# Two leading token blocks of 256, opening loads in order of need, and a copy of W_in within SBUF

## The chip, the cores and the metric

The kernel runs on one core of a Trainium2 chip. The metric is the device time in microseconds. The span of a profile (first to last instruction) is about 1.8 us shorter than the time that is reported for the same run. A ratio is the mean time of one kernel's fast runs over the mean of the other kernel's fast runs of the same rounds, so it is not quite the ratio of the medians that are quoted.

## The reference

The reference is a causal convolution of 7 taps per token and head, then a two-layer network with exact GELU, on 32,768 tokens of 192 channels.

```python
w = softmax(weight)                         # 8 heads x 7 taps
out[b, s] = sum_k w[head, k] * x_pad[b, s + k]   # zeros before the start of each sequence
h = out.reshape(32768, 192) @ w_in          # 192 x 2048
g = 0.5 * h * (1 + erf(h / sqrt(2)))
return g @ w_out                            # 2048 x 192
```

## The kernel before

The 32,768 tokens are two halves of 16,384. A block takes 512 tokens of each half; the two halves lie in partitions 0-63 and 64-127, and so every TensorE instruction comes in pairs that run side by side (in the trace of this kernel the two of a pair start 3 to 4 ns apart; the 512-column ones take 376 ns each). There are 32 blocks. For each block the sync engine loads `x`; VectorE transposes it (3 steps), convolves it (21 steps: 7 taps times 3 groups of 64 channels) and writes `xc` as bf16; TensorE multiplies with W_in, 128 columns at a time ("first matmuls"); ScalarE applies GELU; TensorE multiplies with W_out ("second matmuls"); VectorE evicts the result; the sync engine stores it.

Stage n, in this document, is TensorE's pass that has the first matmuls of block n and, between them, the second matmuls of block n - 1. A slice is the part of a stage that belongs to one ScalarE call of 1,024 elements.

```python
# GpSimd: W_in (cast to bf16) after three instructions that build `sel`; then W_out
for c0, c1, s in ((0, FC, S_WIN[0]), (FC, F, S_WIN[1])):      # FC = 512 of F = 2048 columns
    for hf in range(2):                                        # lower and upper 64 partitions
        g.dma_start(win[64*hf.., c0:c1], w_in[..]).then_inc(s, 16)
g.dma_start(wout, w_out).then_inc(S_WOUT, 16)
# ...
# VectorE: block 0 alone, then block n + 1 with the evictions of block n - 1 between its steps
for op in ops0: run(0, op)
for n in range(NSB + 1):
    if n >= 2: evac(n - 2, 3)
    # ... 24 steps of block n + 1 in three parts, evac(n - 1, 0..2) after each
# ScalarE: one call per slice
a.wait_ge(S_MM1, u + 1)
a.activation(out=gT[n % 2][:, i*2*TB:(i+1)*2*TB], in_=hp[u % 2][:, :], func=AF.Gelu)
# TensorE
for n in range(NSB):
    for i in range(NF):                       # 16 slices
        mm1(n, i)                             # 6 matmuls, 512 columns
        if n >= 1: mm2_run(n - 1, ...)        # 16 matmuls
t.wait_ge(S_GELU, NF * NSB)                   # all of the last block, then its second matmuls
# ...
# Sync: the taps' weights, then x of blocks 0, 1, 2 ... without waiting
sp.dma_start(wsb, weight)
load(0); load(1)
# ... load(n + 2) and the stores
```

(Cuts are marked with `# ...`; access patterns are shortened.)

Of the kernel before, what the change touches and what calls it, by code (L numbers as in the profile page):

```python
# [11 lines left out]
def bass_lightweight_conv__then__act_gelu_exact_kernel(  # L12
# [16 lines left out]
    TB = 512  # L29
    assert B % 2 == 0 and SEQ % TB == 0  # L30
    NSB = HALF // TB
    SPB = SEQ // TB
# [3 lines left out]
    MB = TB // 32  # L36
# [4 lines left out]

# [6 lines left out]
    outt = out.tensor  # L48

# [14 lines left out]
    with es:  # L64
# [10 lines left out]
        xin = [sbt("xin%d" % i, [128, MB * XC], F32) for i in range(NX)]  # L75
# [9 lines left out]
        S_WIN = [sem("S_WIN%d" % i) for i in range(2)]  # L85
        S_WOUT = sem("S_WOUT")
        S_XIN = [sem("S_XIN%d" % i) for i in range(NX)]
        S_OUT = [[sem("S_OUT%d_%d" % (i, j)) for j in range(2)] for i in range(2)]
# [19 lines left out]
        def _(g):  # L108
            g.memset(sel[:, :], 1.0).then_inc(S_SEL)
# [21 lines left out]
            for c0, c1, s in ((0, FC, S_WIN[0]), (FC, F, S_WIN[1])):  # L131
                for hf in range(2):
                    g.dma_start(  # L133
                        ap(win, 64 * hf * NP * F + c0, [[NP * F, 64], [F, NP], [1, c1 - c0]]),
                        ap(wint, c0, [[F, 64], [64 * F, NP], [1, c1 - c0]]),
                    ).then_inc(s, 16)
# [4 lines left out]
            for n in range(NSB):  # L141
                dst = ap(xT[n % 2], 0, [[NP * XW, 128], [XW, NP], [1, HL]])
                if n >= 2:
                    g.wait_ge(S_CV, NCV * (n - 1))
                if n % SPB == 0:
                    g.memset(dst, 0.0).then_inc(S_HALO)  # L146
                else:
                    g.wait_ge(S_TR, NP * n)
                    g.tensor_copy(  # L149
                        dst,  # L150
                        ap(xT[(n - 1) % 2], TB, [[NP * XW, 128], [XW, NP], [1, HL]]),
                    ).then_inc(S_HALO)

        @block.vector
        def _(v):
# [16 lines left out]
            def trans(n, p):  # L172
                if p == 0:
                    v.wait_ge(S_XIN[n % NX], 64 * (n // NX + 1))  # L174
                    if n >= 2:
                        v.wait_ge(S_CV, NCV * (n - 1))
                    if n >= 1:
                        v.wait_ge(S_HALO, n)
                v.transpose(  # L179
                    ap(xT[n % 2], p * XW + HL, [[NP * XW, 128], [1, TB]]),  # L180
                    ap(xin[n % NX], 64 * p, [[MB * XC, 128], [XC, MB], [1, 32]]),
                ).then_inc(S_TR)

            def conv(n, k, p):
                if k == 0 and p == 0:
                    v.wait_ge(S_TR, NP * (n + 1))
                    v.wait_ge(S_HALO, n + 1)
                idx = NCV * n + NP * k + p
                if idx >= NP:
                    v.wait_ge(S_CV, idx - NP + 1)  # L190
                src = ap(xT[n % 2], p * XW + k, [[NP * XW, 128], [1, TB]])
                w = wcol[:, p * KS + k : p * KS + k + 1]
                a = acc[:, p * TB : (p + 1) * TB]
                if k == 0:
                    ins = v.tensor_scalar(a, src, w, None, ALU.mult)  # L195
                else:
                    dst = a
                    if k == KS - 1:
                        dst = xc[n % 2][:, p * TB : (p + 1) * TB]
                        if n >= 2 and p == 0:  # L200
                            v.wait_ge(S_MM1, NF * (n - 1))
                    ins = v.scalar_tensor_tensor(  # L202
                        dst, src, w, a, op0=ALU.mult, op1=ALU.add
                    )
                ins.then_inc(S_CV)

            def evac(m, g):
                v.wait_ge(S_MM2, 4 * m + g + 1)
                if m >= 2 and g % 2 == 0:
                    v.wait_ge(S_OUT[m % 2][g // 2], 16 * (m // 2))  # L210
                v.tensor_copy(  # L211
                    ap(osb[m % 2], 2 * g * C, [[8 * C, 128], [C, 2], [1, C]]),
                    ap(ob[g % 2], 0, [[1024, 128], [512, 2], [1, C]]),
# [14 lines left out]
            for n in range(NSB + 1):  # L228
                ops = list(ops0) if n + 1 < NSB else []
                cut = [0, 9, 17, 24, 24]  # L230
                if n >= 2:
                    evac(n - 2, 3)
                for q in range(4):
                    for op in ops[cut[q] : cut[q + 1]]:
                        run(n + 1, op)
                    if n >= 1 and q < 3:
                        evac(n - 1, q)
            evac(NSB - 1, 3)

        @block.scalar  # L240
        def _(a):
            a.wait_ge(S_PRO, 1)
# [7 lines left out]
            for n in range(NSB):  # L250
                for i in range(NF):
                    u = n * NF + i
                    a.wait_ge(S_MM1, u + 1)
                    if i == 0 and n >= 2:
                        a.wait_ge(S_MM2, 4 * (n - 1))
                    a.activation(  # L256
                        out=gT[n % 2][:, i * 2 * TB : (i + 1) * 2 * TB],
# [5 lines left out]
        def _(t):  # L263
# [8 lines left out]
            ins.then_inc(S_PEP)  # L272

            def mm1(n, i):
                u = n * NF + i
# [4 lines left out]
                if n == 0 and i == 0:  # L280
                    t.wait_ge(S_WIN[0], 32)
                if n == 0 and 128 * i == FC:
                    t.wait_ge(S_WIN[1], 32)
                for p in range(NP):
                    for hf in range(2):
                        r = slice(64 * hf, 64 * hf + 64)
                        ins = t.matmul(  # L287
                            hp[u % 2][:, hf * TB : (hf + 1) * TB],
                            win[r, p * F + 128 * i : p * F + 128 * i + 128],
                            xc[n % 2][r, p * TB : (p + 1) * TB],  # L290
                            start=(p == 0),
                            stop=(p == NP - 1),
                            tile_position=(64 * hf, 0),
                        )
                ins.then_inc(S_MM1)

            def mm2_run(m, g, ph, i0, i1):


                if g >= 2 or m >= 1:  # L300
                    if ph == 0 and i0 == 0:
                        t.wait_ge(S_EV, 4 * m + g - 1)
                if ph == 1 and i0 == 0:
                    t.wait_ge(S_PH, 4 * m + g + 1)
                for i in range(i0, i1):
                    for hf in range(2):
                        sub = ph ^ hf
                        s = 2 * g + sub
                        r = slice(64 * hf, 64 * hf + 64)
                        c0 = i * 2 * TB + s * 128  # L310
                        ins = t.matmul(  # L311
                            ob[g % 2][:, 512 * sub : 512 * sub + C],
                            gT[m % 2][r, c0 : c0 + 128],
                            wout[r, i * C : (i + 1) * C],
                            start=(ph == 0 and i == 0),
                            stop=(ph == 1 and i == NF - 1),
                            tile_position=(64 * hf, 0),
                        )
                if i1 == NF:
                    ins.then_inc(S_MM2 if ph == 1 else S_PH)  # L320

            for n in range(NSB):
                for i in range(NF):
                    mm1(n, i)
                    if n >= 1:
                        if n == 1 and i == 0:
                            t.wait_ge(S_WOUT, 16)
                        if i < 2:
                            t.wait_ge(S_GELU, NF * (n - 1) + 8 * (i + 1))
                        g, r = divmod(i, 4)  # L330
                        mm2_run(n - 1, g, r // 2, 8 * (r % 2), 8 * (r % 2) + 8)
            m = NSB - 1
            t.wait_ge(S_GELU, NF * NSB)
            for g2 in range(2):
                for ph in range(2):
                    for g in range(2):
                        mm2_run(m, 2 * g2 + g, ph, 0, NF)

        @block.sync
        def _(sp):  # L340
            sp.dma_start(wsb[:, :], ap(wt, 0, [[KS, H], [1, KS]])).then_inc(S_WSB, 16)  # L341

            def load(n):
                if n >= NX:
                    sp.wait_ge(S_TR, NP * (n - NX + 1))
                for q in range(4):
                    off = ((q // 2) * HALF + n * TB) * D + 32 * (q % 2)
                    sp.dma_start(  # L348
                        ap(xin[n % NX], 32 * q * MB * XC, [[MB * XC, 32], [XC, MB], [1, XC]]),
                        ap(xt, off, [[D, 32], [32 * D, MB], [1, XC]]),  # L350
                    ).then_inc(S_XIN[n % NX], 16)

            def store(m, hf):
                sp.wait_ge(S_EV, 4 * m + 2 * hf + 2)
                sp.dma_start(
                    ap(outt, (hf * HALF + m * TB) * C, [[C, 128], [128 * C, 4], [1, C]]),
                    ap(osb[m % 2], hf * 4 * C, [[8 * C, 128], [C, 4], [1, C]]),
                ).then_inc(S_OUT[m % 2][hf], 16)

            load(0)  # L360
            load(1)
            for n in range(NSB + 2):
                if n + 2 < NSB:
# [3 lines left out]
                if 1 <= n <= NSB:  # L367
                    store(n - 1, 0)
            for s in range(2):
                for hf in range(2):  # L370
                    sp.wait_ge(S_OUT[s][hf], 16 * ((NSB + 1 - s) // 2))

# [27 lines left out]
```

## Time and profile before

| | before |
|---|---|
| time, median of the 4 runs taken beside the changed kernel | 712.8 us (712.34 to 714.07) |
| span of the profiled run | 710.9 us |
| first transpose of block 0 | 14.84 us |
| first W_in matmul | 30.06 us |
| stage 1 starts (steady state) | 47.27 us |
| stage 2 starts | 68.20 us |

Two lines of the page: busy time of each engine with its share of the span, and the shares of the chain of work that ended last.

```profile
PE 676.3 (95%) x11270; PEld 487.9 (69%) x11270; DVE 544.5 (77%) x901; ACT 526.2 (74%) x516; POOL 18.2 (3%) x44
PE 94%; DVE 2%; DMA 2%; ACT 2%; issue 0%; SPq 0%; DVEq 0%
```

PE is TensorE, DVE is VectorE, ACT is ScalarE, POOL is GpSimd. TensorE sets the time, and only the rest, about 35 us (710.9 - 676.3), can be won without changing its work. The timeline shows where that rest lies. Its columns are the start (us), the length (us), engine, line, operation, output and inputs with their shapes, the number of instructions merged, and in brackets the idle time before them and what ended it.

```profile
14.84 1.90 DVE L179 STREAM_TRANSPOSE xT<-xin 128x512 f32<-128x512 f32 x3 [9.67 <-DMA xin<-in_x_dram]
16.78 1.30 DVE L195 TENSOR_SCALAR acc<-xT,wcol 128x512 f32<-128x512 f32 x3
18.00 10.02 DVE L202 SCALAR_TENSOR_TENSOR acc<-xT,wcol,acc 128x512 f32<-128x512 f32 x15
27.93 2.07 DVE L202 SCALAR_TENSOR_TENSOR xc<-xT,wcol,acc 128x512 bf16<-128x512 f32 x3
30.06 7.26 PE L287 MATMUL hp<-xc,win 64*128 64x512 bf16 x36 [25.10 <-DVE xc L202]
...
68.20 0.81 PE L287 MATMUL hp<-xc,win 64*128 64x512 bf16 x6
...
694.50 0.81 PE L287 MATMUL hp<-xc,win 64*128 64x512 bf16 x6
695.14 0.82 PE L311 MATMUL ob<-wout,gT 64*128 64x192 bf16 x16
696.43 10.73 PE L311 MATMUL ob<-wout,gT 64*128 64x192 bf16 x256 [0.46 <-ACT gT L256]
```

VectorE waits 9.67 us for block 0's `x`, works 15.2 us on it, and only then has TensorE something to do. From 68.20 us a slice follows a slice every 1.3075 us, (694.50 - 68.20) / 479, to the end. The windows view gives busy time by stretch; the columns after the length are busy us and instruction count of PE, PEld (weight loads), DVE, ACT and POOL, then the granted clock, the DMA share and GB/s.

```profile
15.00:30.06 15.06, 0.00 (x1) 0.01 (x2) 15.02 (x25) 0.00 (x0) 0.20 (x1) 1.00 1.26 224
30.06:36.50 6.44, 6.38 (x30) 1.58 (x31) 6.41 (x12) 4.11 (x5) 0.45 (x1) 1.00 1.22 195
36.50:47.30 10.80, 9.06 (x68) 2.35 (x70) 10.77 (x18) 10.78 (x12) 0.31 (x1) 1.00 0.14 24
47.30:68.20 20.90, 20.90 (x352) 15.21 (x354) 14.29 (x24) 16.63 (x17) 0.14 (x1) 1.00 0.43 82
```

In the second row TensorE is busy all the time with only 30 matmuls, 5 slices of 1.29 us; a slice of first matmuls alone takes 0.65 us later. I read this as half clock: the slices take twice as long, as does one of 1.28 us in the changed kernel's trace (46.26 to 47.54 us), where the clock record reads 0.50. The column of the granted clock still reads 1.00 there, because the trace's first clock record of this run is at 36.07 us. In the third row ScalarE is busy throughout and sets the pace, and in the fourth TensorE is.

### The profile page before, as it was taken

To read this page: it belongs to the slowest core of one execution; us is meant where nothing else is said; L and a number is where in the kernel's file an instruction comes from. 1 tells how busy PE (TensorE), PEld (TensorE's weight loads), DVE (VectorE), ACT (ScalarE), POOL (GpSimd) and SP (SyncE) were. 2 spreads that over 40 slices of the span, in tenths; PEclk is the share of its full clock that TensorE was granted. 3 is DMA by queue.
4 is the path that set the end of the run, shared out by engine and by line. 5 is a ranking of instruction groups with operands and counts; after the bars stand their busy time and mean duration, and the time that the engine had idled before them with its cause. 6 is when DMAs were issued, how large, how long until landed. Compare 5 with 4: busy or idle time off the path is not lost.

```text
span 710.9 us, 24500 instructions
## 1 busy us (share of the span) xinstructions
PE 676.3 (95%) x11270; PEld 487.9 (69%) x11270; DVE 544.5 (77%) x901; ACT 526.2 (74%) x516; POOL 18.2 (3%) x44
## 2 busy tenths in 40 slices
PE   0389999999999999999999999999999999999997
PEld 0037777777777777777777777777777777777776
DVE  2987897777789777779877778977777887777711
ACT  1197777777777777777777777777777777777771
POOL 3000000000000000000000000000000000000000
PEclk9999999999999999999999999999999999999999
DMA  9915533555543455554345555335555433551012
GB/s 188 216 25 119 98 85 83 99 120 121 98 106 86 76 118 121 120 98 94 86 86 120 120 114 98 88 82 102 120 121 98 104 87 75 120 121 46 24 47 68
DMA packets 104390, 71.04 MB, mean 100 GB/s; under 512 B 5216, under 2 KB 103904, under 8 KB 104288
## 3 DMA queue, kind: packets, MB, share of 16 engines
q1 hardware_dynamic: 101392, 67.12, 45.5%
q0 software_dynamic: 2896, 2.36, 2.1%
q8 instruction: 88, 1.44, 0.9%
q14 instruction: 14, 0.11, 0.1%
HBM read 46.66 MB, written 25.17 MB: 101 GB/s over the span
## 4 chain that ended last, share of the span: by engine, by line
PE 94%; DVE 2%; DMA 2%; ACT 2%; issue 0%; SPq 0%; DVEq 0%
PE ob L311 47%; PE hp L287 46%; DMA xin<-in_x_dram 2%; ACT gT L256 2%; DVE acc L202 1%; DVE xT L179 0%; SPq L348 0%; DVE acc L195 0%; DVE xc L202 0%; DVE osb L211 0%; SPq L341 0%; DVEq L174 0%
## 5 line engine op out<-in xcount | busy, mean ns | idle before, releaser
L256 ACT ACTIVATE gT<-hp 128x1024 bf16<-128x1024 f32 x512 | 523.2, 1023 | 169.1 <-PE hp L287 169.1
L287 PE MATMUL hp<-xc,win 64*128 64x512 bf16 x3072 | 417.7, 378 | 26.9 <-DVE xc L202 25.1
L311 PEld LDWEIGHTS ob<-wout,gT 64*128 64x128 bf16 x8192 | 352.6, 94 | 118.2 <-ACT gT L256 0.7
L311 PE MATMUL ob<-wout,gT 64*128 64x192 bf16 x8192 | 419.2, 243 | 0.5 <-ACT gT L256 0.5
L202 DVE SCALAR_TENSOR_TENSOR acc<-xT,wcol,acc 128x512 f32<-128x512 f32 x480 | 325.6, 747 | 0.0
L287 PEld LDWEIGHTS hp<-xc,win 64*128 64x128 bf16 x3072 | 141.3, 94 | 97.3 <-DVE xc L202 25.2
L211 DVE COPY osb<-ob 128x384 f32<-128x384 f32 x128 | 71.0, 555 | 148.2 <-PE ob L311 148.2
L179 DVE STREAM_TRANSPOSE xT<-xin 128x512 f32<-128x512 f32 x96 | 60.4, 681 | 9.7 <-DMA xin<-in_x_dram 9.7
L202 DVE SCALAR_TENSOR_TENSOR xc<-xT,wcol,acc 128x512 bf16<-128x512 f32 x96 | 66.4, 749 | 0.0
L195 DVE TENSOR_SCALAR acc<-xT,wcol 128x512 f32<-128x512 f32 x96 | 40.9, 483 | 1.1
L149 POOL COPY xT<-xT 128x18 f32<-128x18 f32 x28 | 12.3, 438 | 576.3 <-DVE xT L179 576.3
L267 PE MATMUL ob<-wnm,sel 8*128 8x7 f32 x6 | 1.4, 354 | 3.5 <-DVE wnm L165 3.5
L267 PEld LDWEIGHTS ob<-wnm,sel 8*128 8x128 f32 x6 | 1.4, 321 | 3.5 <-issue 3.5
L133 POOL DMA_DIRECT2D win<-in_moe_w_in_dram x4 | 2.6, 657 | 0.0
L243 ACT ACT_TABLE_LOAD x1 | 1.3, 1283 | 0.8 <-PEq L385 0.8
L157 DVE TENSOR_REDUCE wmx<-wsb 8x1 f32<-8x7 f32 x1 | 0.1, 148 | 2.2 <-DMA wsb<-in_weight_dram 2.2
L146 POOL MEMSET xT<- 128x18 f32 x4 | 0.5, 121 | 41.0 <-DVE xc L202 41.0
L169 DVE COPY wcol<-ob 128x21 f32<-128x21 f32 x1 | 0.2, 181 | 1.6 <-PE ob L267 1.6
L256 ACT ACT_TABLE_LOAD x1 | 1.3, 1283 | 0.0
L137 POOL DMA_DIRECT2D wout<-in_moe_w_out_dram x1 | 1.2, 1192 | 0.0
L112 POOL TENSOR_SCALAR_AFFINE_SELECT sel<-sel 8x384 f32<-8x384 f32 x1 | 0.5, 537 | 0.1
L122 POOL TENSOR_SCALAR_AFFINE_SELECT sel<-sel 8x384 f32<-8x384 f32 x1 | 0.5, 532 | 0.1
(10 smaller groups left out, 1.8 us busy)
## 6 DMA issues: line engine op xcount, KB each, us to landing
xin<-in_x_dram SPq DMA_DIRECT2D x128, 320.0 KB, 6.7
out_dram<-osb SPq DMA_DIRECT2D x64, 384.0 KB, 3.0
win<-in_moe_w_in_dram POOLq DMA_DIRECT2D x2, 576.0 KB, 12.7
wout<-in_moe_w_out_dram POOLq DMA_DIRECT2D x1, 768.0 KB, 22.7
win<-in_moe_w_in_dram POOLq DMA_DIRECT2D x2, 192.0 KB, 8.4
wsb<-in_weight_dram SPq DMA_DIRECT2D x1, 0.2 KB
```

The source lines that it names most:

```text
L133: g.dma_start(ap(win, 64 * hf * NP * F + c0, [[NP * F, 64], [F, NP], [1, c1 - c0]]), ap(wint, c0, [[F, 64], [64 * F, NP], [1, c1 - c0]]),) ...
L137: g.dma_start(ap(wout, 0, [[NF * C, 128], [C, NF], [1, C]]), ap(woutt, 0, [[C, 128], [128 * C, NF], [1, C]]),).then_inc(S_WOUT, 16)
L149: g.tensor_copy(dst, ap(xT[(n - 1) % 2], TB, [[NP * XW, 128], [XW, NP], [1, HL]]),).then_inc(S_HALO)
L179: v.transpose(ap(xT[n % 2], p * XW + HL, [[NP * XW, 128], [1, TB]]), ap(xin[n % NX], 64 * p, [[MB * XC, 128], [XC, MB], [1, 32]]),).then_i ...
L195: ins = v.tensor_scalar(a, src, w, None, ALU.mult)
L202: ins = v.scalar_tensor_tensor(dst, src, w, a, op0=ALU.mult, op1=ALU.add)
L211: v.tensor_copy(ap(osb[m % 2], 2 * g * C, [[8 * C, 128], [C, 2], [1, C]]), ap(ob[g % 2], 0, [[1024, 128], [512, 2], [1, C]]),).then_inc(S_EV)
L243: a.activation(out=wex[:, :], in_=wsb[:, :], func=AF.Exp, bias=wmx[:, 0:1], accum_out=wsm[:, 0:1],).then_inc(S_ACTP)
L256: a.activation(out=gT[n % 2][:, i * 2 * TB : (i + 1) * 2 * TB], in_=hp[u % 2][:, :], func=AF.Gelu,).then_inc(S_GELU)
L267: ins = t.matmul(ob[0][:, p * KS : (p + 1) * KS], sel[:, p * 128 : (p + 1) * 128], wnm[:, :],)
L287: ins = t.matmul(hp[u % 2][:, hf * TB : (hf + 1) * TB], win[r, p * F + 128 * i : p * F + 128 * i + 128], xc[n % 2][r, p * TB : (p + 1) * T ...
L311: ins = t.matmul(ob[g % 2][:, 512 * sub : 512 * sub + C], gT[m % 2][r, c0 : c0 + 128], wout[r, i * C : (i + 1) * C], start=(ph == 0 and i ...
```

## The change

The intent is to give TensorE its first work earlier. The first two blocks take 256 tokens per half; to keep ScalarE's calls at 1,024 elements, two 128-column chunks of W_in share one call. The loads are ordered by need: block 0's `x` alone on the sync queue, the taps' weights on ScalarE's, the first quarter of W_in first on GpSimd's; block 1's `x` waits for block 0's; the upper half of the rest of W_in is copied from the lower half within SBUF, ahead of block 2's `x`. Two further differences come with the rewriting: the evictions are placed differently between VectorE's steps, and TensorE's wait for the last block's activations is split into two halves.

```diff
+    WS = [256, 256] + [512] * ((HALF - 512) // 512)      # OFF, NCH, NSL, SL0, NG, G0 follow from it
 # GpSimd
+            for hf in range(2):                           # now ahead of the memset and the two selects
+                g.dma_start(win[64*hf.., 0:FC], w_in[..]).then_inc(S_WIN[0], 16)
             g.memset(sel[:, :], 1.0).then_inc(S_SEL)
 ...
-            for c0, c1, s in ((0, FC, S_WIN[0]), (FC, F, S_WIN[1])):
-                for hf in range(2): g.dma_start(...).then_inc(s, 16)
+            g.dma_start(win[lower 64.., FC:F], w_in[..]).then_inc(S_WIN[1], 16)
 # VectorE
-                cut = [0, 9, 17, 24, 24]
+                for g in range(ng):
+                    to = min(len(ops), (len(ops) * (g + 1) + ng - 2) // max(ng - 1, 1))
+                    ... steps of block n + 1 up to `to`, then evac(n - 1, g); the last one in the next stage
 # ScalarE
+            a.dma_start(wsb[:, :], ap(wt, 0, [[KS, H], [1, KS]])).then_inc(S_WSB, 16)
-                        out=gT[n % 2][:, i * 2 * TB : (i + 1) * 2 * TB],
+                        out=ap(gT[n % 2], i * c * 2 * w, [[NF * 2 * TB, 128], [w, 2], [2 * w, c], [1, w]]),
 # TensorE
+                for cc in range(c):                       # c = 2 chunks of W_in per slice in a small block
-            t.wait_ge(S_GELU, NF * NSB)                   # before the last second matmuls
+                    if i % max(c, 8) == 0: t.wait_ge(S_GELU, ...)   # for each half of the chunks
 # Sync
             load(0)
+            sp.wait_ge(S_XIN[0], 64)
             load(1)
+            sp.wait_ge(S_WIN[1], 16)
+            sp.dma_start(win[upper 64.., FC:F], win[lower 64.., FC:F]).then_inc(S_WIN[2], 16)
+            load(2)
```

## The prediction

> **What bounds the kernel now.** TensorE: the page gives PE 95% busy, the chain of waits puts 94% on it. In the timeline the steady stage (one block's first matmuls beside the previous block's second) takes 20.9 us, (694.7 - 47.3) / 31, PE without a gap, ScalarE about 16.4, VectorE 17.0. The change leaves that work as it is; what it can win lies before. VectorE waits until 14.84 us for block 0's x; transposes and convolution take 15.2 us; PE's first W_in matmul starts at 30.06; stage 0 starts with slices of 1.29 us, then runs at ScalarE's pace (a call per 0.97 us) to 47.3. The second steady stage starts at 68.2.
>
> **What the change does.**
> 1. Block 0's x is half as large and goes first. Before, its first 1,024 x packets, as many as the new block has, had landed at 7.1 us. Now its queue starts 0.5 us earlier, though W_in's packets begin near 4.4 us (3.6 after issue, as before). VectorE starts at about 6.8 instead of 14.8: -8 us.
> 2. Block 0 has 256 columns. VectorE steps at 512 are 0.631 (transpose), 0.433 (first tap), 0.668 us (later taps). [...] First matmul at about 16 us: -14.
> 3. Two small blocks cost 18.5 us of VectorE where one cost 15.2: +3.3 us. Block 2 (512) follows at 15.2. Until the steady state VectorE sets the pace. ScalarE's calls stay 1,024 wide.
> 4. Block 2's x queues behind block 1's and the SBUF copy of W_in. From the packet rates (300 per us alone, 220 beside W_out) I estimate landing near 27 us, when VectorE is free at 25.3-26: +1 to 1.5 us.
> 5. PE's small stages end near 37 us, but block 2 is convolved only at 42. [...] This trace shows 1.29 us slices for 6.4 us after the opening idle; I count 1.2 us for a partial repeat.
>
> **On the critical path.** Block 3's stage, the first steady one, starts at 6.8 + 18.5 + 1.5 + 15.2 = 42, plus stage 2 (block 3's convolution and two evictions, 16.4; ScalarE 15.5), plus 1.2 = about 59.8 us. From there 30 full stages and the tail remain, as after 68.2 before. Gain 8.4 us, not 14, because VectorE gives much back. The late copy of W_in (near 18.5 us) should hit the third slice of stage 0 and cost nothing: PE has slack there.
>
> **Predicted time:** 704.3 us, range 700.5 to 708.0. Faster by over 2%: 3%; within 2%: 96%; slower by over 2%: 1%. For 2% the steady state would have to start before 54 us; after a start at 6.8, two small and two large blocks (48.9 us of VectorE) do not allow it.
>
> **What would show it.** In the timeline: first transpose at 6-7.5 us; 256-wide taps spaced near 0.40 us; first W_in matmul at 15.5-17; PE waiting several us for VectorE before block 2, with slices of over 1 us after it; block 3's first matmul at 58-62; stages of 20.9 us after it; PE busy time nearly unchanged.
>
> **What would make it wrong.** x of block 1 or 2 landing much later; the copy or W_out landing after 25 us; [...] eviction order stalling the first second matmuls; 256-wide weight loads not hidden.

The sum came to 6.8 + 18.5 + 1.5 + 15.2 = 42.0 us, plus 16.4 for stage 2, plus 1.2 for its slow slices: 59.6, put as "about 59.8". The gain is 68.2 - 59.8 = 8.4 us, and 704.3 is 712.7 (the kernel before, median of the three runs then made) less 8.4. The 18.5 (two small blocks; with half of it the first matmul at about 16 us) and the spacing of 0.40 us were estimates; the changed kernel measured 18.6 us and 0.40 us. The 1.2 was from the 1.29 us slices; that the clock would fall after the gap was not shown by the trace at hand. Stage 2 then lost 1.2 to 1.3 us. The third cut is a case of what would make the forecast wrong.

## The result, and the profile after

| | before | after |
|---|---|---|
| time, median of 4 runs each | 712.8 us | 705.1 us (704.3 to 705.92) |
| ratio of the fast runs | | 0.9889, 95% interval 0.9871 to 0.9907 |
| span of the profiled run | 710.9 us | 702.9 us |
| first transpose | 14.84 us | 9.35 us |
| first W_in matmul | 30.06 us | 18.61 us |
| first steady stage that leaves 30 full stages | 68.20 us (stage 2) | 60.98 us (stage 3) |

The gain of about 1.1% is outside the interval. The two lines of the page:

```profile
PE 676.9 (96%) x11366; PEld 518.1 (74%) x11366; DVE 550.2 (78%) x925; ACT 526.5 (75%) x516; POOL 17.9 (3%) x44
PE 93%; DMA 3%; DVE 2%; SPq 0%; issue 0%; POOL 0%; POOLq 0%
```

TensorE's busy time is what it was. The timeline of the changed kernel:

```profile
9.35 1.10 DVE L193 STREAM_TRANSPOSE xT<-xin 128x256 f32<-128x256 f32 x3 [3.34 <-DMA xin<-in_x_dram]
...
11.30 6.01 DVE L221 SCALAR_TENSOR_TENSOR acc<-xT,wcol,acc 128x256 f32<-128x256 f32 x15
...
18.61 6.43 PE L333 MATMUL hp<-xc,win 64*128 64x256 bf16 x60 [12.81 <-DVE xc L221]
18.85 1.10 DVE L193 STREAM_TRANSPOSE xT<-xin 128x256 f32<-128x256 f32 x3 [0.34 <-DMA xin<-in_x_dram]
...
28.38 1.90 DVE L193 STREAM_TRANSPOSE xT<-xin 128x512 f32<-128x512 f32 x3 [0.40 <-DMA xin<-in_x_dram]
...
43.66 0.82 PE L333 MATMUL hp<-xc,win 64*128 64x512 bf16 x6 [4.02 <-DVE xc L221]
...
60.98 0.83 PE L333 MATMUL hp<-xc,win 64*128 64x512 bf16 x6
61.62 0.84 PE L365 MATMUL ob<-wout,gT 64*128 64x192 bf16 x16
...
687.27 0.83 PE L333 MATMUL hp<-xc,win 64*128 64x512 bf16 x6
687.91 11.40 PE L365 MATMUL ob<-wout,gT 64*128 64x192 bf16 x272
```

The first matmul comes 11.45 us earlier, but only 7.2 us of it are left at the first steady stage. What takes them back is in the middle: VectorE spends 9.2 us on each small block, then 15.3 us on block 2, and TensorE, which ended stage 1 at 39.6 us, waits 4.02 us for it. From 60.98 on, slices follow every 1.3075 us as before, (687.27 - 60.98) / 479. The windows from the end of stage 1 on:

```profile
39.60:43.66 4.06, 0.04 (x1) 0.03 (x1) 4.06 (x7) 0.45 (x1) 0.00 (x0) 1.00 0.00 0
43.66:49.30 5.64, 5.63 (x58) 3.72 (x60) 5.61 (x11) 3.24 (x4) 0.45 (x1) 0.70 0.68 167
49.30:61.00 11.70, 11.70 (x174) 7.58 (x170) 10.66 (x17) 11.70 (x13) 0.00 (x0) 1.00 0.40 70
61.00:81.90 20.90, 20.90 (x357) 15.93 (x355) 17.06 (x28) 16.65 (x17) 0.45 (x1) 1.00 0.88 164
```

After the gap the granted clock is 0.70 on average over 5.64 us. The trace's clock record is sharper: half clock from 44.94 to 48.35 us, 3.41 us long. The end of the kernel is about 0.7 us shorter as well: from the last slice of first matmuls to the end of the span it was 16.4 us (694.50 to 710.88) and is 15.7 us (687.27 to 702.93). The wait of 0.46 us before the last 256 matmuls is gone; 16 and 256 now run on as 272.

The theory after this reading is a theory of pacing: the opening is one chain, from the landing of block 0's `x` over VectorE's work on blocks 0, 1 and 2 to stage 2, and nothing else in the change matters for the time except the split wait at the end. Its rival is a theory of order: the order of the loads and the copy of W_in make most of the gain.

The profile's own chain of the changed kernel already differs from the theory in one place (start, length, what):

```profile
4.30 7.74 DMA win<-in_moe_w_in_dram
12.07 0.70 SPq L431
14.09 1.43 SPq L406
15.57 12.79 DMA xin<-in_x_dram
29.02 1.27 DVE xT L193 x2
```

It does not pass over VectorE's work on blocks 0 and 1. It passes over the third load of W_in, which the sync queue (SPq) awaits before the copy (L431) and before block 2's `x` (L406), and over the landing of that `x`, which came 0.40 us after VectorE was free. Up to block 2 there are thus two paths of nearly the same length, VectorE's and that of the loads.

### The profile page after: what moved, and what is told of

Same layout as the page of the kernel before. It is cut to its first block, busy times and chain, and to the rows that moved or that the text cites. A ratio compares the mean times of both kernels' runs of the same rounds, so it can differ in the third digit from the quotient of the medians.

```text
span 702.9 us, 24699 instructions
## 1 busy us (share of the span) xinstructions
PE 676.9 (96%) x11366; PEld 518.1 (74%) x11366; DVE 550.2 (78%) x925; ACT 526.5 (75%) x516; POOL 17.9 (3%) x44
## 4 chain that ended last, share of the span: by engine, by line
PE 93%; DMA 3%; DVE 2%; SPq 0%; issue 0%; POOL 0%; POOLq 0%
PE ob L365 47%; PE hp L333 46%; DMA xin<-in_x_dram 2%; DVE acc L221 1%; DMA win<-in_moe_w_in_dram 1%; SPq L406 0%; POOL win L117 0%; DVE xT L193 0%; DVE acc L214 0%; DVE xc L221 0%; SPq L431 0%; DVE osb L230 0%; POOL sel L124 0%; POOL sel L134 0%; POOL sel L121 0%
## 5 line engine op out<-in xcount | busy, mean ns | idle before, releaser
L289 ACT ACTIVATE gT<-hp 128x1024 bf16<-128x1024 f32 x512 | 523.6, 1024 | 161.2 <-PE hp L333 161.2
L365 PEld LDWEIGHTS ob<-wout,gT 64*128 64x128 bf16 x8192 | 368.9, 94 | 103.2 <-issue 0.7
L333 PE MATMUL hp<-xc,win 64*128 64x512 bf16 (+1 forms) x3168 | 426.9, 373 | 18.1 <-DVE xc L221 16.8
L365 PE MATMUL ob<-wout,gT 64*128 64x192 bf16 x8192 | 428.9, 243 | 0.0
L221 DVE SCALAR_TENSOR_TENSOR acc<-xT,wcol,acc 128x512 f32<-128x512 f32 (+1 forms) x495 | 327.4, 730 | 0.0
L333 PEld LDWEIGHTS hp<-xc,win 64*128 64x128 bf16 x3168 | 163.1, 95 | 73.4 <-issue 18.5
L221 DVE SCALAR_TENSOR_TENSOR xc<-xT,wcol,acc 128x512 bf16<-128x512 f32 (+1 forms) x99 | 66.8, 730 | 0.0
L193 DVE STREAM_TRANSPOSE xT<-xin 128x512 f32<-128x512 f32 (+1 forms) x99 | 60.8, 665 | 4.1 <-DMA xin<-in_x_dram 4.1
L214 DVE TENSOR_SCALAR acc<-xT,wcol 128x512 f32<-128x512 f32 (+1 forms) x99 | 41.4, 474 | 1.2
```

The source lines that it names most:

```text
L193: v.transpose(ap(xT[n % 2], p * XW + HL, [[NP * XW, 128], [1, w]]), ap(xin[n % NX], 64 * p, [[TB // 32 * XC, 128], [XC, w // 32], [1, 32]] ...
L214: ins = v.tensor_scalar(a, src, wk, None, ALU.mult)
L221: ins = v.scalar_tensor_tensor(dst, src, wk, a, op0=ALU.mult, op1=ALU.add)
L289: a.activation(out=ap(gT[n % 2], i * c * 2 * w, [[NF * 2 * TB, 128], [w, 2], [2 * w, c], [1, w]],), in_=hp[u % 2][:, :], func=AF.Gelu,).th ...
L333: ins = t.matmul(hp[u % 2][:, hf * TB + cc * w : hf * TB + cc * w + w], win[r, p * F + f0 : p * F + f0 + 128], xc[n % 2][r, p * TB : p * T ...
L365: ins = t.matmul(ob[gg % 2][:, 512 * sub : 512 * sub + C], gT[m % 2][r, c0 : c0 + 128], wout[r, i * C : (i + 1) * C], start=(ph == 0 and i ...
```

## The experiments

Eleven runs (ten altered kernels, and the changed kernel again) were made in three groups, each group on one chip with its own runs of the kernel before (medians 713.45, 712.86 and 714.0 us). Since these differ, compare ratios across groups. All kernels are built from the changed one, and all were correct but one. The stages are those of one profiled run each, which need not be the median run.

| run | median us | ratio to before | first steady stage |
|---|---|---|---|
| changed kernel, first time | 705.1 | 0.9889 | 60.98 us |
| loads_only | 711.4 | 0.9970 | (stage 1) 46.6 us |
| blocks_only | 704.84 | 0.9879 | 59.25 us |
| late_win | 704.79 | 0.9881 | 61.67 us |
| win_hbm | 704.72 | 0.9874 | 60.75 us |
| keep_warm | 703.47 | 0.9867 | 60.24 us |
| unpaired | 704.77 | 0.9887 | 59.36 us |
| short_conv (wrong result) | 698.75 | 0.9801 | 55.24 us |
| four_small | 706.8 | 0.9911 | not the same stage |
| again (changed kernel) | 705.08 | 0.9881 | 61.26 us |
| tail_one_wait | 706.01 | 0.9893 | 61.29 us |
| all_small | 701.13 | 0.9821 | not the same stage |

### loads_only: the new loads without the small blocks

```diff
-    WS = [256, 256] + [512] * ((HALF - 512) // 512)
+    WS = [512] * (HALF // 512)
```

> The changed kernel's loads, but all blocks of 512. Pacing theory (the gain is the time from block 0's x to the convolution of the first full blocks; loads alone cannot shorten it): block 0's x is 2,048 packets again, shares the engines with W_in's early packets (130 per us instead of 300) and lands near 15 us as before; first W_in matmul near 30 us, time 711.5 to 713.0 (only about 0.6 us saved at the end, where the wait for the last activations is split in two). Rival, order theory (loads in order of need and the copy of W_in make most of the gain): below 709.

Measured: 711.4 us, ratio 0.997 (0.9956 to 0.9984). The first transpose is at 14.41 us, the first W_in matmul at 29.67 us. The time is just below the range expected by the pacing theory and far above the 709 us of the order theory. In the profiles the span fell from 710.9 to 709.6 us, and about half of that is the split wait at the end (see tail_one_wait). The ratio is worth 2.1 us (1.1 to 3.1 by its interval). Without the 0.6 us of the split wait, the order of the loads and the new placement of the evictions, which is in this run too, give together 0.5 to 2.5 us of the 7.9 us that the whole change gives: not most of it.

### blocks_only: the small blocks with the old loads

```diff
-            (GpSimd: first quarter of W_in ahead of the selects, lower half of the rest after them)
+            (GpSimd: all four loads of W_in from memory after the selects, then W_out)
-            load(0); wait for it; load(1); wait for W_in; copy of W_in; load(2)
+            wsb; load(0); load(1); load(2)
```

> The small blocks with the loads as in the kernel before (W_in after the selects, both halves from memory, x not held back). Pacing theory: block 0's x lands near 7.2 us instead of 9.3, block 2's x near 26.7 instead of 28.3, so block 2's convolution ends about 1.5 us earlier: first steady stage near 59.3 us (60.98 in the changed kernel), time 703.0 to 704.5, that is faster than the whole change. Order theory: the reordering is needed, time above 707.

Measured: 704.84 us, ratio 0.9879 (0.9861 to 0.9898). This is not above 707, so the reordering is not needed. It is not clearly faster than the whole change either: the medians are within the scatter. The time is just above the range expected (704.5 us), although the first steady stage came at 59.25 us as expected; the profiled run, 702.98 us, is the fastest of the four. Block 0's `x` was there at 7.72 us (7.2 expected), but block 1's `x`, whose packets here run beside all of W_in's, came only at 18.9 us (in the kernel before, with the same loads of W_in, 288 or 289 packets of `x` start per microsecond from 4 to 6 us, and 57 to 81 from 10 to 16 us, beside W_in's), when VectorE had waited 2.0 us for it, and block 2 started at 27.99 us, 0.4 us earlier than in the changed kernel. What was won at block 0 was lost at block 1.

### late_win: the first quarter of W_in issued later

```diff
-            (first two loads of W_in)                      # ahead of the memset and the selects
             g.memset(halo_memset, 0.0).then_inc(S_HALO)
+            (first two loads of W_in)
```

> The changed kernel with the first two W_in loads issued after GpSimd's selects instead of first. If step 1 missed because W_in's packets share the engines with block 0's x: first transpose near 7.2 us instead of 9.35, first W_in matmul near 16.5 us, but block 2's x, held behind the chain of loads, then is the limit (lands 26.5 to 27.5), time 703.3 to 704.6. If the miss was the x queue itself: first transpose stays above 9 us and the time at 705.

Measured: 704.79 us, ratio 0.9881 (0.9859 to 0.9902). The timeline of this run shows VectorE's first steps of blocks 0, 1 and 2:

```profile
6.85 1.10 DVE L193 STREAM_TRANSPOSE xT<-xin 128x256 f32<-128x256 f32 x3 [1.29 <-DMA xin<-in_x_dram]
16.66 1.10 DVE L193 STREAM_TRANSPOSE xT<-xin 128x256 f32<-128x256 f32 x3 [0.65 <-DMA xin<-in_x_dram]
27.92 1.90 DVE L193 STREAM_TRANSPOSE xT<-xin 128x512 f32<-128x512 f32 x3 [2.13 <-DMA xin<-in_x_dram]
```

The first transpose moved from 9.35 to 6.85 us, so step 1 of the prediction missed because W_in's packets run beside those of block 0's `x`. In the changed kernel W_in's first packet starts at 2.92 us; 399 packets of `x` start in the microsecond before it, and in the four microseconds from there 109 to 137 packets of `x` start per microsecond; in this run it starts at 4.30 us, and in the two microseconds before 437 and 334 packets of `x` start. But the 2.5 us do not arrive, and the time is 0.2 us above the range expected: block 2's `x` lands at 27.9 us here too, and VectorE waits 2.13 us for it. The opening has two limits at nearly the same place, VectorE and the delivery of block 2's `x`, and taking away one shows the other. The run to run scatter is large here, 703.24 to 707.54 us, and it follows the mean granted clock for each run: 1.000 in the run of 703.24 us, 0.997 and 0.998 at 704.79 and 704.53, 0.995 at 705.48, 0.993 at 707.54. The profiled run, at 0.995, had 6.83 us of half clock after its gap. The four runs of the changed kernel part in the same way: 704.3 and 704.69 us at 0.997 and 0.998, 705.51 and 705.92 us at 0.995.

### win_hbm: no copy within SBUF

```diff
-            g.dma_start(win[lower 64.., FC:F], w_in[..]).then_inc(S_WIN[1], 16)
+            for hf in range(2):
+                g.dma_start(win[64*hf.., FC:F], w_in[..]).then_inc(S_WIN[1 + hf], 16)
-            load(1); wait for S_WIN[1]; copy of W_in; load(2)
+            load(1); load(2)
```

> The changed kernel, but the upper copy of the rest of W_in is loaded from memory too, no copy within SBUF, and block 2's x is not held back by it. Pacing theory: block 2's x lands a little earlier, but VectorE is free only at 28.0 us, so at most 0.5 us is won; W_in and W_out land later without harm: 704.3 to 705.3. Order theory: the copy relieves the load engines, so its loss costs over 1 us: above 706.

Measured: 704.72 us, ratio 0.9874 (0.9859 to 0.989), block 2's first matmul at 43.44 us (43.66 in the changed kernel). The copy within SBUF is worth nothing here. It saves reading 1.18 MB from memory, but the saving is off the chain.

### keep_warm: TensorE kept busy through the gap

```diff
+                if n == 2 and i == 0:
+                    for d in range(18):
+                        for hf in range(2):      # pairs, as all matmuls here; overwritten by the next ones
+                            t.matmul(hp[u % 2][:, hf*TB:(hf+1)*TB], win[r, 0:128], win[r, 0:TB], start=True, stop=True, ...)
                 if i == 0:
                     t.wait_ge(S_CV, NCV * (n + 1))
```

> The changed kernel with 18 pairs of throw-away matmuls (512 columns, about 3.9 us at full clock) in TensorE's wait before block 2; the next real matmul overwrites what they write. [...] no slice of over 1 us after block 2's start, stage 2 takes 15.5 to 16 us instead of 17.3, first steady stage near 59.5 us (then set by block 3's convolution, which ended at 59.49 us), time 703.3 to 704.2, and the runs lie closer together. If they come from something else (loads of W_in or W_out, the first evictions): unchanged, 705.

The first of the two causes: TensorE's clock falls in the gap, for which the changed kernel's record of 0.50 from 44.94 to 48.35 us spoke.

Measured: 703.47 us (703.06 to 704.01), ratio 0.9867 (0.9851 to 0.9884). The windows of this run, from its throw-away matmuls on:

```profile
39.30:44.17 4.87, 4.05 (x42) 1.91 (x38) 4.87 (x9) 0.57 (x1) 0.00 (x0) 1.00 0.02 3
44.17:60.20 16.03, 15.81 (x224) 9.36 (x224) 15.99 (x27) 15.17 (x16) 0.45 (x1) 1.00 0.55 107
```

The throw-away matmuls take 4.06 us (39.29 to 43.35). The clock stays at 1.00 and no slice is slow: stage 2 takes 16.1 us (44.17 to 60.24) instead of 17.3. Here VectorE is busy for 15.99 of 16.03 us, and the first steady stage waits 0.25 us for block 3's convolution: with the half clock gone, VectorE again sets the pace. The first steady stage came at 60.24 and not at 59.5 us, because in this run block 0's `x` landed 0.6 us later than in the changed kernel's profiled run. The scatter fell from 1.6 us (four runs of the changed kernel) to 1.0 us, but win_hbm, with half clock after its gap, has 0.8 us, so four runs are too few to show this. The intervals of the ratios overlap (0.9871 to 0.9907 for the changed kernel); it is the traces that show the half clock as the cause of the slow slices: in the changed kernel 30 matmuls fall into the 3.41 us at 0.50 and 50 into the 3.41 us after them, and here, at 1.00, no slice is slow. The size of its effect on stage 2 is about 1.2 to 1.3 us.

### unpaired: one ScalarE call per chunk of W_in

```diff
-    NCH = [TB // w for w in WS]
+    NCH = [1 for w in WS]
-                        in_=hp[u % 2][:, :],
+                        in_=ap(hp[u % 2], 0, [[2 * TB, 128], [TB, 2], [1, c * w]]),
```

> The changed kernel with one ScalarE call per 128-column chunk of W_in in the small blocks too: 16 calls of 512 elements instead of 8 of 1,024, about 0.6 us each by estimate. Pacing theory: ScalarE and TensorE have slack before block 2, so stages 0 and 1 grow by 1 to 3 us but block 2 starts at the same 43.5 us: time 704.3 to 705.6, perhaps with a shorter gap and less slow clock. Rival (the pairing is what makes small blocks affordable): above 706.5.

Measured: 704.77 us, ratio 0.9887 (0.9868 to 0.9906): no difference. The calls of 512 elements took 0.60 us each, as estimated. Block 2's first matmul is at 43.39 us, after a gap of 2.57 us. In the profiled run the clock did not fall after this shorter gap (the first slice's first matmuls take 0.64 us, 43.39 to 44.03), and that run, 703.18 us, is the fastest of the four (granted clock 0.999; the others have 0.997 to 0.998 and took 704.67 to 705.21 us). The pairing of chunks costs nothing and brings nothing.

### short_conv: less VectorE work in block 2

```diff
+                    if n == 2 and 1 <= k <= 3:       # 9 of the 21 steps on 2 columns
+                        src = ap(xT[n % 2], p * XW + k, [[NP * XW, 128], [1, 2]])
+                        dst = a = acc[:, p * TB : p * TB + 2]
```

> Wrong result on purpose: in block 2 alone nine of VectorE's 21 convolution steps cover 2 columns instead of 512, about 4.7 us less. If VectorE's work on the first full block is on the critical path: block 2's first matmul at 39.6 to 40 us right behind stage 1, no gap, no slow slices, first steady stage near 55.3 us, time 699.0 to 700.3. If TensorE or loads set the pace: within 1 us of 705.

Measured: 698.75 us (698.43 to 699.2), ratio 0.9801 (0.9785 to 0.9817). The result is wrong (relative error 0.11). The timeline around the start of stage 2:

```profile
38.54 0.83 PE L368 MATMUL ob<-wout,gT 64*128 64x192 bf16 x15
39.20 0.38 PE L336 MATMUL hp<-xc,win 64*128 64x512 bf16 x1
39.21 0.24 PE L368 MATMUL ob<-wout,gT 64*128 64x192 bf16 x1
39.30 0.81 PE L336 MATMUL hp<-xc,win 64*128 64x512 bf16 x5
```

Block 2's first matmul follows stage 1 without a gap, and the first steady stage is at 55.24 us. VectorE was done with block 2 after 10.3 us (28.56 to 38.83) instead of 15.05 us (28.38 to 43.43), that is 4.8 us less, and the kernel became about 6 us faster, because the gap and the half clock after it went together (granted clock 1.000). This shows that VectorE's work on the first full block is on the critical path.

### four_small: four blocks of 256

```diff
-    WS = [256, 256] + [512] * ((HALF - 512) // 512)
+    WS = [256] * 4 + [512] * ((HALF - 1024) // 512)
```

> Four leading blocks of 256 instead of two, all else as in the changed kernel. Pacing theory: a small stage gives TensorE 10.5 us against VectorE's 9.2 plus about 1 of evictions, so the two keep step once running; block 2's convolution ends near 37.6 us, behind stage 1's end at 39.6, stages 2 and 3 end near 60.8, and the one gap comes before the first full block (conv ends near 63). By my sum of TensorE's idle time 2.5 us less: 702 to 703.5. If small blocks cost more than they bring: above 705.

Measured: 706.8 us (705.8 to 707.55), ratio 0.9911 (0.9894 to 0.9927). This expectation missed: slower than the change, not faster. The timeline of VectorE and, in the last line, of TensorE:

```profile
36.81 0.55 DVE L230 COPY osb<-ob 128x384 f32<-128x384 f32 x1
38.78 0.56 DVE L230 COPY osb<-ob 128x384 f32<-128x384 f32 x1 [1.42 <-PE ob L365]
39.26 1.09 DVE L193 STREAM_TRANSPOSE xT<-xin 128x256 f32<-128x256 f32 x3
...
49.30 0.56 DVE L230 COPY osb<-ob 128x384 f32<-128x384 f32 x1 [0.45 <-PE ob L365]
49.78 1.89 DVE L193 STREAM_TRANSPOSE xT<-xin 128x512 f32<-128x512 f32 x3
...
65.05 1.47 PE L333 MATMUL hp<-xc,win 64*128 64x512 bf16 x6 [5.26 <-DVE xc L221]
```

In VectorE's program, evictions stand between the blocks. Before the one at 38.78 us it waited 1.42 us for second matmuls, although the next block's `x` had landed by 27.75 us, so with this order it cannot run ahead of TensorE; in my sum it did. The first full block (here block 4) thus starts at 49.78 us, TensorE waits 5.26 us for it, and after this longer gap the clock record shows 6.83 us of half clock, twice that of the changed kernel. More small blocks only move the gap, as long as a full block follows.

### again, tail_one_wait and all_small

The changed kernel was run again beside the next two, for a comparison on one chip.

> The changed kernel unaltered, beside the next two on the same chip: 704.3 to 706.0, with slow slices after block 2's start and a first steady stage between 60 and 62 us.

Measured: 705.08 us, with half clock from 43.79 to 47.20 us in the profiled run, 3.41 us again, and the first steady stage at 61.26 us.

In tail_one_wait the old wait for all of the last block's activations is put back:

```diff
             m = NB - 1
+            t.wait_ge(S_GELU, SL0[NB])
```

> The changed kernel with the old wait for all of the last block's activations put back before the last second matmuls. If 0.6 us of the gain comes from the split wait at the end: TensorE idle 0.4 to 0.5 us before its last 256 matmuls (none in the changed kernel), time 0.6 us above that of the run beside it, which the interval may not show but the trace must. If the tail's gain was chance: no idle time there.

Measured: 706.01 us against 705.08 beside it; the ratios' intervals overlap (0.9893, 0.9875 to 0.991, against 0.9881, 0.9862 to 0.99). The timeline shows the wait itself:

```profile
687.58 0.82 PE L333 MATMUL hp<-xc,win 64*128 64x512 bf16 x6
688.23 0.84 PE L365 MATMUL ob<-wout,gT 64*128 64x192 bf16 x16
689.52 10.73 PE L365 MATMUL ob<-wout,gT 64*128 64x192 bf16 x256 [0.46 <-ACT gT L289]
```

From the last slice's first matmul to the start of the last 256 it is 1.94 us here, 1.93 us in the kernel before and, with the split wait, 1.30 us (0.64 us to the second matmuls, 0.66 us for the 16 that belong to the slice). So 0.6 us of the gain come from the end of the kernel.

All_small takes the lesson of four_small to its end: if the step from small to full blocks makes the gap, have no full blocks.

```diff
-    WS = [256, 256] + [512] * ((HALF - 512) // 512)
+    WS = [256] * (HALF // 256)
```

> All 64 blocks of 256. The run with four small blocks missed because evictions in VectorE's program order held block 3's convolution back, and because the wait (5.3 us) and the slow clock came again at the first full block. With no full block there is no such wait: first stage with second matmuls at 28 us as there, then 63 stages of 10.52 us (measured there), end of them near 690.8, then 128 second matmuls, 5.3 us, and about 4 us to the end: span near 700, time 701 to 702.5, faster than the changed kernel by about 3.5 us. If VectorE (9.05 plus 1.1 of evictions of 10.52 us) cannot hold this pace, or weight loads for 256 columns show: above 704.

Measured: 701.13 us (700.8 to 701.42), ratio 0.9821 (0.9805 to 0.9838), against 705.08 us of the changed kernel beside it. It beats both kernels. The timeline of VectorE in mid-run:

```profile
300.86 0.56 DVE L230 COPY osb<-ob 128x384 f32<-128x384 f32 x1
301.86 0.56 DVE L230 COPY osb<-ob 128x384 f32<-128x384 f32 x1 [0.45 <-PE ob L365]
302.33 1.09 DVE L193 STREAM_TRANSPOSE xT<-xin 128x256 f32<-128x256 f32 x3
...
312.86 1.09 DVE L193 STREAM_TRANSPOSE xT<-xin 128x256 f32<-128x256 f32 x3
```

VectorE needs all but 0.45 us of a stage of 10.52 us (302.33 to 312.86), and TensorE still sets the pace. The steady state begins at 28.13 us. A slice takes 1.315 us, (689.57 - 28.13) / 503, instead of 1.3075, which costs about 3.8 us over the run; the missing gap and the earlier steady state bring more than that.

## Why the prediction was right

The predicted time was 704.3 us, the measured one 705.1. The sum to the first steady stage, term by term in us:

| term | predicted | measured | from |
|---|---|---|---|
| block 0's `x` there | 6.8 | 9.35 | first transpose |
| two small blocks | 18.5 | 18.6 | 9.35 to 27.98, with 0.34 of wait |
| wait for block 2's `x` | 1.5 | 0.4 | bracket at 28.38 |
| block 2 to its first matmul | 15.2 | 15.3 | 28.38 to 43.66 |
| stage 2 with the slow clock | 17.6 | 17.3 | 43.66 to 60.98 |
| first steady stage | about 59.8 | 60.98 | |
| gain at the end | 0 | 0.7 | tail, 0.6 of it the split wait |

- Step 1 (block 0's `x`) was mis-sized by 2.5 us. The prediction took W_in's first packets to come 3.6 us after issue, as before; they came 1.6 us after it (1.31 to 2.92 us), and while they ran 109 to 137 `x` packets started per microsecond, against 399 in the microsecond before. late_win showed this cause, and showed as well that the 2.5 us cost the kernel almost nothing, because block 2's `x` would then be the limit. The first transpose and the first W_in matmul lie outside the stretches that the prediction gave as signs (6 to 7.5 and 15.5 to 17 us).
- Step 2 (cost of a small block) was right: steps of 0.40 us, 9.2 us per block. What the estimate rested on is cut from the forecast; the trace now shows the cost: 256 columns fewer make a later tap 0.27 us shorter (0.668 to 0.40), not half as long (0.33).
- Step 3 (VectorE sets the pace until the steady state) was right from block 2 on, and short_conv showed it: 4.8 us less VectorE work in that block took about 6 us off the time. For blocks 0 and 1 it is not shown: in late_win VectorE was through with them 2.2 us earlier (25.79 instead of 27.98 us), and block 2 began only 0.5 us earlier.
- Step 4 (block 2's `x` near 27 us) was 1.4 us too early, but VectorE was later too, so its wait was smaller than predicted. In the prediction and in the run alike block 2 starts when its `x` lands, so these 1.4 us are in substance the error of the first steady stage (59.8 predicted, 60.98 measured). That step 1's larger miss did not add to it is luck: VectorE was late by about as much as block 2's `x`.
- Step 5 (idle gap and half clock) was right in kind and size: a gap of 4.0 us (the prediction's 37 to 42 makes 5) and 1.2 to 1.3 us lost. The clock records show half clock of 3.41 us in five of the profiled runs (both of the changed kernel, win_hbm, tail_one_wait, and blocks_only, there before block 1) and of 6.83 us in two (late_win and four_small). What the forecast gave as the cause of the fall was not shown by its trace; which gaps the half clock followed in the runs is in the last section. keep_warm took the half clock away.
- The late W_in cost TensorE nothing, as predicted: no wait of TensorE for it stands in the timeline of the changed kernel. The profile's chain passes over its landing only because the sync queue awaits it before block 2's `x`; in win_hbm, without that wait, block 2's first matmul came 0.2 us earlier.
- What the prediction did not see is the end of the kernel: the split wait, 0.6 us (tail_one_wait). It hid about half of the 1.2 us by which the first steady stage came late.

What stays open: why single runs with an equal granted clock still differ (702.98 and 705.36 us at 0.997 in blocks_only), and why block 2's `x` lands between 27.4 and 28.4 us with four different orders of the loads (win_hbm, late_win, blocks_only and the changed kernel). The same bytes have to pass in each, but no run took W_out away to show it.

## What to carry to other kernels

When a pipeline's first item is made smaller to start earlier, add up the work of the engine that feeds it until the first full-sized item is through, and set beside it when that item's input lands; the step from small to full size returns as a gap a part of what the early start brought, and half clock may follow the gap (here 3.41 us of it after a gap of 4.02 us). Ask whether the small size can be kept throughout: here it fits by 0.45 us per stage, and it was better than the two mixes that were run. A load that is moved to the front can slow whatever was in front before (here `x`, from 399 packets started per microsecond to 109 to 137 beside W_in's), and removing one wait at the start shows the next one, so read each wait's bracket before counting its whole length as gain.

## What the traces showed of the clock and of the loads

- Half clock followed gaps of different length: in the second run of the changed kernel the clock fell 2.5 us after TensorE's last matmul (41.28 to 43.79 us), and in blocks_only 2.15 us after it (25.84 to 27.99 us, before block 1), while after a gap of 2.57 us in unpaired it did not fall. So in these runs the length of the gap alone did not decide. In the changed kernel's trace the clock changes at whole multiples of 3.41 us from the first clock record (first record at 24.46 us; half clock from 44.94 us, six of them later, to 48.35 us, seven). Of such stretches, it fell after one with 1.27 us of TensorE work (changed kernel, 41.53 to 44.94 us), and did not after one with 1.58 us (unpaired, 41.56 to 44.97 us) or one with 1.53 us (changed kernel, 38.11 to 41.53 us). No run was made to test this further.
- Stage 2 lost 1.2 to 1.3 us with 3.41 us of half clock (changed kernel: 17.3 us, against 16.0 to 16.1 without) and about 2.5 us with 6.83 us (late_win: 18.5 us).
- W_in's first packet started 1.6 us after issue in the changed kernel, 1.9 us in late_win, 2.0 us in blocks_only and 3.6 us in the kernel before.
- The 640-byte packets of `x` fell from 399 started in the microsecond before W_in's first packet to 109 to 137 per microsecond beside W_in's casting load (changed kernel).
